# First batch of an attention-then-ReGLU kernel: first scores moved into the gate ring, z sums in banks of their own, two thirds of the gate-and-value table formed beside the first units

## Chip, cores, metric

One core of a Trainium2 chip. The time is the device time of a run in microseconds (us); the span in a profile is about 1.8 us shorter. Every run also has a mean granted TensorE clock.

## The reference, cut

```python
# x: 4 x 12416 x 128, inducing: 32 x 128 (m = 32)
def mab(q, kv):                       # softmax attention, scale = 1/sqrt(128)
    s = scale * (q @ kv.transpose(0, 2, 1))
    a = np.exp(s - s.max(-1, keepdims=True))
    a /= a.sum(-1, keepdims=True) + 1e-09
    return a @ kv
h = mab(I, x)                         # 32 summary rows of a batch
y = mab(x, h).reshape(49664, 128)
gate = np.maximum(y @ w_gate, 0.0)    # 128 x 1536
val = y @ w_val
out = (gate * val) @ w_out            # 1536 x 128
```

## The kernel before

The kernel never forms y. It forms h, folds h into the weights (hgv = h times w_gate and w_val, 1536 columns, made in three parts of 512), and multiplies hgv by the exps p of the second scores. The work after that goes in *slots*, one *unit* of 1024 gated columns a slot: two gate matmuls into two banks of the ring "g", two value matmuls into a two-bank tile of "v", two relus by ScalarE (ACT), one multiply gate times value by VectorE (DVE). Unit s of a pair needs columns 128 s to 128 s + 127 of hgv only. Batches 1 to 3 have their first phase hidden beside units of the batch before; batch 0 has nothing to hide behind, and its start is what the change is about. That first phase takes x in 14 parts as they land: cast to fp16, transpose by PE, first scores (inducing rows times x), their exp, and from the exps the z sums (the denominators of the softmax) and the h sums; hT is h over z, transposed. A "ring" is a set of PSUM banks taken in turn, "fillers" are matmuls whose result nobody reads. PE below is TensorE, POOL is GpSimd.

```python
def bank(tag, name, shape=None, dtype=FP32):          # eight PSUM banks in all
    return psum.tile(shape or [P, BLK], dtype, tag=tag, bufs={"g": 3, "v": 2, "o": 1}[tag], name=name)

z1_ps = bank("v", "z1_ps", [P, 2 * BLK])               # one two-bank tile for both z sums
z1a, z1 = z1_ps[:, 0 : 8 * M], z1_ps[:, BLK : BLK + M]
s1_ps = bank("v", "s1_ps", [P, 2, 2 * TPB, 2 * M])     # first scores: one two-bank tile, halves in turn
...
for j in range(n_parts + 3):                           # 14 parts of x as they land
    # cast of part j (POOL and ACT)
    if 1 < j < n_parts + 2:                            # scores and exp of part j - 2
        ps = s1_ps[:, j % 2, :, 0:M]
        for t in range(t0, t1):
            nc.tensor.matmul(ps[:, t - t0, :], xTs(xT, t, 1), indT, start=True, stop=True)
        nc.scalar.activation(out=p1[:, 0 : t1 - t0, :], in_=ps[:, 0 : t1 - t0, :], func=AF.Exp, scale=sm_scale)
    # z and h sums of part j - 3; turn(j): PE transpose into ring "g", DVE copy out of it
    ...
idle(idle_ps, 3, xT[0][:, 0:4, :].rearrange("p t c -> p (t c)"))   # filler matmuls
hT = finish_h(hT_ps, z1)                               # reciprocal of z, then h / z, on DVE
s2 = s2_pe(hT, xT, (0, 1, 0, 1)); p2 = s2_exp(s2)
ps = hgv_pe(hT, 0)                                     # four matmuls; then DVE copies two halves
for a in (0, BLK // 2):
    nc.vector.tensor_copy(out=hgv[:, a : a + BLK // 2], in_=ps[:, a : a + BLK // 2])
ps = bank("v", "hgv_ps", [P, 2 * BLK])
for k in (1, 2):
    hgv_pe(hT, k, ps[:, (k - 1) * BLK : k * BLK])
nc.vector.tensor_copy(out=hgv[:, BLK : 2 * BLK], in_=ps[:, 0:BLK])
nc.scalar.copy(out=hgv[:, 2 * BLK : DFF], in_=ps[:, BLK : 2 * BLK])
...
while True:                                            # the slots; "at" is the slot's number
    unit = next(todo_units, None); window.append(unit)
    ready = None if at == 10 else window.pop(0)        # values and multiply run a slot later, from 10 on two
    # gates of unit, values of ready, posted work, one filled-in event, output chain
    if 0 < at < 10:
        idle(idle_ps, 2, hgv[:, 0:BLK])                # two fillers a slot, meant to keep PE's clock up
    # relus of unit (ACT), multiply of ready (DVE)
    at += 1
```

The softmax here doesn't subtract the row's maximum and nothing guards it: scores larger than these inputs give would overflow.

## Time and profile before

Three runs gave 709.27 to 711.6 us, with a median of 710.46. The profile lines are in the prediction below; this table, from the busy time by stretches, gives what matters.

| stretch, us | PE | DVE | ACT | what goes on |
|---|---|---|---|---|
| 0 to 10 | 40% | 33% | 39% | x begins to land |
| 10 to 20 | 79% | 53% | 68% | casts, transposes, first scores, at the pace of x |
| 20 to 30 | 79% | 53% | 49% | h, hgv, first units |
| 30 to 40 | 99% | 87% | 90% | units, with 3.4 us at half clock |
| 60 to 700 | 91% | 99% | 98% | units at full pace |

To read it: from 40 us on DVE and ACT are full.

### The profile page before, as it was taken

The numbers are of one execution on the slowest core, as the hardware profiler recorded it, in microseconds if no ns is written. First come the engines' busy times: TensorE is split into PE (matmuls) and PEld (weight loads), VectorE is DVE, ScalarE is ACT, GpSimd is POOL, SyncE is SP. The second block draws the span as 40 slices with busy tenths as digits, with TensorE's granted clock in tenths as the row PEclk, the third lists the DMA queues.
The fourth block names the chain that finished last, engine by engine and source line by source line (L and its number), as shares of the span: only waits on it lengthen the run. The fifth ranks groups of instructions, "written<-read, shape, count | busy, mean of one in ns | idle before, by whom it ended". The sixth has DMA issues, their size and how long they took to land.

```text
span 709.0 us, 14077 instructions
## 1 busy us (share of the span) xinstructions
PE 637.9 (90%) x4626; PEld 186.0 (26%) x4626; DVE 678.9 (96%) x621; ACT 675.3 (95%) x1382; POOL 350.5 (49%) x646
## 2 busy tenths in 40 slices
PE   6899999999998999999998899999999898888997
PEld 5322222222222222222222222222222222222224
DVE  4599999999999999999999999999999999999997
ACT  5699999999999999999999999999999999999995
POOL 3661637535176546355256362852616443534543
PEclk9999999999999999999999999999999999999999
DMA  8657865431247867523139677653223132231222
GB/s 342 216 129 163 171 178 152 119 82 61 74 145 152 203 167 199 133 82 91 46 107 197 166 175 172 160 124 76 68 67 94 50 90 56 79 89 49 71 58 89
DMA packets 142346, 87.58 MB, mean 124 GB/s; under 512 B 117152, under 2 KB 125632, under 8 KB 139968
## 3 DMA queue, kind: packets, MB, share of 16 engines
q1 hardware_dynamic: 142272, 86.68, 47.2%
q8 instruction: 36, 0.59, 0.4%
q14 instruction: 38, 0.31, 0.1%
HBM read 27.80 MB, written 25.43 MB: 75 GB/s over the span
## 4 chain that ended last, share of the span: by engine, by line
ACT 32%; PE 29%; issue 17%; DVE 14%; DMA 6%; POOL 1%; SPq 1%; ACTq 0%; DVEq 0%
ACT g L961 23%; DVE gv L966 13%; PE o_ps L662 13%; PE v_ps L864 9%; ACT oT L668 5%; PE g_ps L864 4%; DMA gv<-in_x_dram 2%; ACT p2q L195 2%; DMA x<-in_moe_w_val_dram 1%; ACT p1T L527 1%; DMA out_dram<-osb 1%; DMA x<-in_x_dram 1%; PE h_ps L579 1%; POOL osb L679 0%; PE idle_ps L263 0%
## 5 line engine op out<-in xcount | busy, mean ns | idle before, releaser
L966 DVE TENSOR_TENSOR gv<-g,v_ps 128x1024 f16<-128x1024 f16 (+1 forms) x578 | 658.0, 1210 | 9.4 <-PE g_ps L864 5.9
L961 ACT ACTIVATE g<-g_ps 128x512 f16<-128x512 f32 x1164 | 604.0, 618 | 12.3 <-PE g_ps L864 8.5
L662 PE MATMUL o_ps<-gv,wo 128*128 128x512 f16 x1128 | 352.5, 384 | 43.9 <-ACT oT L668 43.9
L679 POOL TENSOR_SCALAR osb<-o,z2i 128x128 f32<-128x128 f16 x380 | 165.9, 453 | 276.0 <-DMA o<-oT 273.9
L864 PE MATMUL g_ps<-p,hgv 32*128 32x512 f16 x1152 | 284.4, 380 | 2.6 <-ACT g L961 1.9
L864 PE MATMUL v_ps<-p,hgv 32*128 32x512 f16 x1152 | 224.2, 384 | 9.5 <-DVE gv L966 7.9
L864 PEld LDWEIGHTS <-hgv 32*128 32x128 f16 x2400 | 69.5, 91 | 269.3 <-issue 264.7
L662 PEld LDWEIGHTS <-wo 128*128 128x128 f16 x1176 | 80.9, 97 | 211.8 <-issue 195.4
L435 POOL TENSOR_TENSOR z2i<-zt,minus 128x16 f32<-128x16 f32 (+3 forms) x31 | 73.2, 2366 | 0.3
L668 ACT CAST oT<-o_ps 128x512 f16<-128x512 f32 (+1 forms) x98 | 58.4, 596 | 0.0
L496 POOL CAST x<-x 128x2048 f16<-128x2048 f32 x18 | 34.0, 1890 | 18.3 <-DMA x<-in_x_dram 18.3
L428 POOL TENSOR_TENSOR zt<-zt 128x32 f32<-128x32 f32 (+5 forms) x124 | 35.1, 283 | 9.7
L428 POOL TENSOR_TENSOR zt<-p2T 128x256 f32<-128x256 f16 (+3 forms) x31 | 17.4, 563 | 25.9 <-DMA p2T<-p 15.2
L270 DVE COPY xT<-xT_ps 128x1024 f16<-128x1024 f16 (+1 forms) x13 | 8.4, 650 | 10.0 <-PE xT_ps L269 9.2
L269 PE MATMUL xT_ps<-eye,x 128*128 128x128 f16 x97 | 9.0, 242 | 5.5 <-POOL x L281 4.8
L282 ACT CAST x<-gv 128x512 f16<-128x512 f32 (+1 forms) x12 | 7.2, 597 | 6.9 <-DMA gv<-in_x_dram 6.9
L195 ACT ACTIVATE p2q<-s_ps 128x512 f16<-128x512 f32 x22 | 13.4, 610 | 0.0
L281 POOL CAST x<-gv 128x512 f16<-128x512 f32 (+1 forms) x12 | 7.2, 598 | 10.2 <-DMA gv<-in_x_dram 10.1
L527 ACT ACTIVATE p1T<-s1T_ps 128x512 f16<-128x512 f32 x18 | 11.1, 616 | 0.0
L179 PE MATMUL s_ps<-xT,hT 128*32 128x512 f16 x108 | 10.8, 392 | 0.2
L601 POOL TENSOR_TENSOR hp<-hp,hq 128x129 f32<-128x129 f32 (+1 forms) x18 | 8.3, 461 | 2.8 <-ACT hq L600 2.8
L966 DVE TENSOR_TENSOR gvr<-g,v_ps 128x512 f16<-128x512 f16 x12 | 8.0, 684 | 1.7 <-PE g_ps L864 1.7
(93 smaller groups left out, 159.1 us busy)
## 6 DMA issues: line engine op xcount, KB each, us to landing
out_dram<-osb SPq DMA_DIRECT2D x95, 256.0 KB, 2.2
x<-in_x_dram SPq DMA_DIRECT2D x18, 1024.0 KB, 6.0
gv<-in_x_dram SPq DMA_DIRECT2D x11, 512.0 KB, 7.5
p<-p2q SPq DMA_DIRECT2D x88, 64.0 KB, 2.0
o<-oT SPq DMA_TRANSPOSE x98, 2.3
x<-in_moe_w_out_dram SPq DMA_DIRECT2D x1, 768.0 KB, 9.2
gv<-in_x_dram SPq DMA_DIRECT2D x2, 256.0 KB, 10.5
x<-in_moe_w_gate_dram SPq DMA_DIRECT2D x1, 512.0 KB, 9.0
```

The source lines that it names most:

```text
L179: nc.tensor.matmul(ps[32 * r : 32 * r + 32, :], hT[:, 0:M], xTs(xT, blocks[r] * TPB, TPB), start=True, stop=True,)
L195: nc.scalar.activation(out=p2q, in_=ps, func=AF.Exp, scale=sm_scale)
L428: nc.gpsimd.tensor_tensor(out=dst, in0=v[:, :, :, 0:m], in1=v[:, :, :, m : 2 * m], op=ALU.add)
L435: nc.gpsimd.tensor_tensor(out=z2i, in0=v[:, :, :, 0], in1=minus1[:, 0 : n * g].rearrange("p (n g) -> p n g", n=n), op=ALU.pow,)
L496: nc.gpsimd.tensor_copy(out=s["x16"][:, t0:t1, :], in_=s["x32", q])
L527: nc.scalar.activation(out=p1T, in_=ps, func=AF.Exp, scale=sm_scale)
L662: nc.tensor.matmul(c["ps"][:, 0:w], wo[:, i, :], gv(i), start=(i == 0), stop=(i == NFF - 1))
L668: nc.scalar.copy(out=oT[:, 0:w], in_=c["ps"][:, 0:w])
L679: nc.gpsimd.tensor_scalar(out=osb[:, t, :], in0=o16[:, t, :], scalar1=zz, scalar2=zz, op0=ALU.mult, op1=ALU.mult,)
L864: nc.tensor.matmul(ps[:, cols], hgv[:, s * P : (s + 1) * P], p2, start=True, stop=True)
L961: nc.scalar.activation(out=g16[:, k * BLK : (k + 1) * BLK], in_=ps, func=AF.Relu)
L966: nc.vector.tensor_tensor(out=ready["dst"][:, a : a + w], in0=ready["g16"][:, a : a + w], in1=ready["v"][:, a : a + w], op=ALU.mult,)
```

## The change

Intent: take two waits out of the start. The scores no longer share one tile with their predecessors, nor the late z matmuls one with DVE's sum; and only the first third of hgv is made before the first unit, so that unit 0 doesn't wait for the last of w_val. Three fillers take the place of the hgv matmuls, to keep PE busy. The core of the diff (left out: the renaming in the z loop, the old `idle_ps` bank that goes, and the same `ev_hgv` put into the later batches):

```diff
-    z1_ps = bank("v", "z1_ps", [P, 2 * BLK])
-    z1a, z1 = z1_ps[:, 0 : 8 * M], z1_ps[:, BLK : BLK + M]
-    s1_ps = bank("v", "s1_ps", [P, 2, 2 * TPB, 2 * M])
+    z1a_ps = bank("v", "z1a_ps", [P, 2 * BLK])
+    z1a, idle_ps = z1a_ps[:, 0 : 8 * M], z1a_ps[:, BLK : 2 * BLK]
+    z1 = bank("v", "z1_ps", [P, M])
...
-            ps = s1_ps[:, j % 2, :, 0:M]
+            ps = bank("g", "s1_ps", [P, 8, M])
...
+            for t in range(n if j - 3 >= n_big else 0):          # all z matmuls, then all h matmuls
+                first, last = j - 3 == n_big and t == 0, end and t == n - 1
+                nc.tensor.matmul(z1, ones16, p1[:, t, :], start=first, stop=last)
...
-    ps = bank("v", "hgv_ps", [P, 2 * BLK])
-    for k in (1, 2):
-        hgv_pe(hT, k, ps[:, (k - 1) * BLK : k * BLK])
-    nc.vector.tensor_copy(out=hgv[:, BLK : 2 * BLK], in_=ps[:, 0:BLK])
-    nc.scalar.copy(out=hgv[:, 2 * BLK : DFF], in_=ps[:, BLK : 2 * BLK])
+    idle(idle_ps, 3, xT[0][:, 0:4, :].rearrange("p t c -> p (t c)"))
...
+    def ev_hgv(b, k, first, last):
+        def pe(at):
+            ps = hgv_pe(state[b]["hT"], k)                       # a bank of ring "g"
+            post[at + 1].append(lambda: hgv_evac(state[b]["hgv"], ps, k))   # by ACT
+        fill(first, last, pe)
+    ev_hgv(0, 1, 1, 1)
+    ev_hgv(0, 2, 4, 4)
...
-                    ev_s2_quad(b, qd, a + 4, a + 8)
+                    ev_s2_quad(b, qd, a + (4 if a else 12), a + (8 if a else 18))
...
-                ev_s2(b, (b, 1), (2, 3, 2, 3), 5, 8)
+                ev_s2(b, (b, 1), (2, 3, 2, 3), 7, 8)
```

More of the change, by code (lines that the diff above doesn't have):

```diff
@@ L307 @@
                 )
+            end = j == n_parts + 2
+            for t in range(n if j - 3 >= n_big else 0):
+                first, last = j - 3 == n_big and t == 0, end and t == n - 1
+                nc.tensor.matmul(z1, ones16, p1[:, t, :], start=first, stop=last)
             for t in range(n):
-                first, last = j == 3 and t == 0, j == n_parts + 2 and t == n - 1
-                if j - 3 >= n_big:
-                    nc.tensor.matmul(
-                        z1, ones16, p1[:, t, :], start=j - 3 == n_big and t == 0, stop=last
-                    )
+                first, last = j == 3 and t == 0, end and t == n - 1
                 nc.tensor.matmul(hT_ps, x16[:, t0 + t, :], p1[:, t, :], start=first, stop=last)
@@ L319 @@
         if j == n_parts:
-            idle_ps = bank("g", "idle_ps")
             z1s = st([P, M], FP32, "z1s", 1)
@@ L641, in act @@
                 for k in range(3):
-                    def mk(at, k=k):
-                        ps = hgv_pe(s["hT"], k)
-                        post[at + 1].append(lambda: hgv_evac(s["hgv"], ps, k))
-                    fill(at + 2, at + 9 + 3 * k, mk)
+                    ev_hgv(b, k, at + 2, at + 9 + 3 * k)
             post[at + 1].append(act)
```

## The prediction

> **What bounds the kernel now.** I read the page first, then the busy time by stretches, the chain of waits of the first 37 us, and each engine's own timeline from 20 to 37 us. The page's busy shares and the stretches say where time can be lost at all:
>
> ```profile
> PE 637.9 (90%) x4626; PEld 186.0 (26%) x4626; DVE 678.9 (96%) x621; ACT 675.3 (95%) x1382; POOL 350.5 (49%) x646
> ...
> L966 DVE TENSOR_TENSOR gv<-g,v_ps 128x1024 f16<-128x1024 f16 (+1 forms) x578 | 658.0, 1210 | 9.4 <-PE g_ps L864 5.9
> L961 ACT ACTIVATE g<-g_ps 128x512 f16<-128x512 f32 x1164 | 604.0, 618 | 12.3 <-PE g_ps L864 8.5
> ```
>
> ```profile
> 20.00:30.00 10.00, 7.92 (x117) 4.24 (x118) 5.26 (x11) 4.85 (x13) 6.99 (x12) 0.99 0.71 216
> 30.00:40.00 10.00, 9.90 (x58) 2.55 (x55) 8.65 (x8) 8.99 (x20) 4.09 (x5) 0.84 0.33 113
> 40.00:50.00 10.00, 9.32 (x55) 2.39 (x56) 9.89 (x9) 9.94 (x21) 8.38 (x15) 1.00 0.78 193
> ```
>
> Columns of the second: stretch, length, then busy us of PE, PE's weight loads, DVE, ACT and POOL, then the granted PE clock. From 36 us to the end DVE and ACT are both 98% busy (1.17 us a unit of 1024 gated columns): nothing in the diff touches that stretch, except that it may begin earlier. So the whole question is how much earlier the gating stream reaches its full pace. In before that is at 36.2 us: DVE starts units 0 to 5 at 28.65, 30.16, 31.74, 33.25, 34.76 and 36.23, then eight units in 9.40 us, 1.18 each. The chain of waits names what holds the first relu back to 27.95 (start, length, what):
>
> ```profile
> 15.52 9.44 DMA x<-in_moe_w_val_dram
> ...
> 25.01 1.05 POOL wv L326
> ...
> 26.10 0.62 PE hgv_ps L160 x6
> ...
> 26.75 0.70 DVE hgv L338
> ...
> 27.47 0.59 ACT hgv L339
> 28.06 0.51 ACT g L961
> ```
>
> The second and third parts of the gate-and-value table (hgv) wait for the last piece of w_val, then for its cast, four of their matmuls, a DVE copy, and an ACT copy that starts only when DVE's is done. ACT takes its work in order, so the relu of unit 0, which needs the first part of hgv only, stands behind all that. What follows is a second loss:
>
> ```profile
> 28.00:29.00 1.00, 0.39 (x2) 0.09 (x2) 0.35 (x1) 1.00 (x4) 1.00 (x2) 1.00 0.74 107
> 29.00:30.00 1.00, 1.00 (x7) 0.23 (x8) 0.93 (x2) 1.00 (x4) 0.77 (x4) 0.89 0.61 188
> 30.00:31.00 1.00, 1.00 (x9) 0.16 (x6) 0.84 (x1) 1.00 (x3) 0.84 (x3) 0.50 1.02 426
> 31.00:32.00 1.00, 1.00 (x7) 0.19 (x6) 0.65 (x2) 0.42 (x2) 1.00 (x1) 0.50 0.78 328
> 32.00:33.00 1.00, 1.00 (x6) 0.11 (x4) 0.96 (x1) 0.67 (x2) 0.22 (x2) 0.50 0.06 16
> 33.00:34.00 1.00, 1.00 (x11) 0.28 (x8) 0.75 (x1) 0.90 (x2) 1.00 (x1) 0.90 0.00 0
> ```
>
> PE idles from 27.24 to 28.61 (1.36 us, put down to ACT g), and from about 29.8 to 33.2 its granted clock is 0.50. In those 3.4 us the two filler matmuls of a slot take 0.96 us instead of 0.43, and the units come 1.5 us apart, set by PE.
>
> **What the Trainium skill says.** "TensorE: Matmul & The Clock Gate", section "Part 1: The HAM clock gate", says that the clock is halved after too idle a window of about 3.4 us, and that the windows run freely, not from the kernel's start. The trace agrees: one stretch of 3.4 us at 0.50, right after the least busy 3.4 us of PE. "PSUM — Partial Sum Buffer", section "PSUM bank collisions raise a hardware error", says that two engines may not be on one bank at once, even both reading, so software must order them. The trace shows an ordering coarser than that: the ACT copy of hgv waits for DVE's copy of another bank of the same two-bank tile. The first scores do so too, next.
>
> ```profile
> 22.40 0.25 PE L290 MATMUL s_ps<-indT,xT 128*128 128x32 f16 x4 [0.22 <-ACT p L292]
> ...
> 23.28 0.18 PE L311 MATMUL z_ps<-p,ones 128*128 128x32 f16 x1
> ...
> 24.28 0.36 DVE L146 RECIPROCAL rz<-z_ps 128x32 f32<-128x32 f32 x1 [1.05 <-PE hT_ps L314]
> 24.75 0.22 DVE L148 TENSOR_TENSOR hT<-hT_ps,rz 128x64 f16<-128x64 f32 x1
> ```
>
> Scores of a part wait for the exp of the part before (ACT, 21.96 to 22.34), though it reads the other half of the tile; the z matmuls at 23.28 wait for DVE's sum of the other bank (22.80 to 23.22).
>
> **The change, part by part.**
>
> (a) Scores in the gate ring, z in its own tile. Until about 21.5 us the phase is paced by x arriving: POOL waits 10.1 us and ACT 6.9 us for it, so nothing is gained there. The ring of three now has two takers a round; counting back three, the scores wait for the evacuation of the turned rows that they need anyway, and the turned rows wait for an exp that stands on ACT before the cast that they need anyway. No new wait. After 21.5 us I replay the tail: the scores of the last but one part start at 22.03 instead of 22.40; its exp follows the one before, 22.36 to 22.64; the last scores go at 22.75 instead of 23.07, their exp 23.00 to 23.28 (was 23.42 to 23.70); the fp32 z matmul after DVE's sum at 23.17, the last z matmuls about 23.5 to 23.6, finished at 23.76. With z ahead of the h matmuls, rz runs 23.80 to 24.16 and hT is done at 24.49, instead of 24.97: **0.5 us**.
>
> (b) Two thirds of hgv moved into slots 1 and 4. With hT at 24.49, s2 goes at 24.54 (was 25.02), its exp ends at 25.59, and the first half of the DVE copy of hgv ends about 25.6 (25.69 + 0.38 - 0.48). The three new filler matmuls (3 x 0.215 = 0.65 us) fit exactly from 24.97 to 25.62, so the gate matmuls of unit 0 go at 25.65, the relu at about 26.05, and DVE starts unit 0 about 26.7 instead of 28.65: **1.9 us, of which 1.45 are (b)**. The second part of hgv is now asked for only after the second relu, about 27.1, when wv (cast done at 26.05) is ready: the w_val transfer leaves the chain.
>
> (c) Start-up pace. ACT now has relus of 0.51 us each (six took 3.05 us), plus one evacuation of about 0.5 us in slots 2 and 5. PE is busy most of the time from 26 to 29 us, so I expect no stretch at half clock. Then, following ring and engines by hand: DVE units 0 to 5 start at 26.7, 28.65, 29.9, 31.1, 32.3 and 33.5: from unit 2 on DVE itself is the pace, at 1.22. Unit 5 is **2.7 us** earlier than its 36.23.
>
> (d) What is given back. DVE loses one copy of 0.69 us, and ACT gains it as one more evacuation (two instead of one, about 0.5 us of its pipe). The exp of s2 and of the quad (0.5 to 0.6 us each), done before unit 6 in the kernel before, now come in slots 8 and 13 to 19. So at unit 6 ACT has about 1.1 us more before it than at the same unit in before. If DVE alone bound from there, nothing of it would count; if ACT alone, all. From 36.02 us ACT gave 19 relus in 9.44 us, 0.50 each (one lasts 0.6, but the next starts inside it), so 1.0 us a unit against DVE's 1.18: over the ten units of slots 6 to 15, without an output chain to evacuate, that leaves ACT some 1.8 us in hand, enough for the 1.1; later the two engines are level. I charge **0.3 us**, for what ACT may not make up in time.
>
> Sum: 2.7 - 0.3 = 2.4 us. 710.46 - 2.4 = **708.1 us**, 0.34% less.
>
> **Rivals.**
>
> 1. ACT is the real bound after slot 6, so the postponed exps cost their full 1.1 us: gain 1.6, time 708.9. For it: ACT is 98% busy, level with DVE. Against: the 1.8 us in hand worked out above.
>
> 2. The clock falls anyway, because the windows run freely and the new order still makes PE wait for relus of 0.5 us. Then some three or four units come 1.5 us apart again: 3 to 4 x 0.3 = about 1 us back, time 709.1. Against it: seven banks of gates and hgv matmuls, three fillers and two more each slot keep PE streaming some 75% of 26 to 28 us by my replay, as against less than 60% of before's 26.4 to 29.8. The other way round, before may escape the low clock in some runs; its three times (709.27 to 711.6) spread by about that much.
>
> 3. The shared gate ring adds waits in the phase of loading, or the second part of hgv takes a bank that the relus need: 0.5 to 1 us lost, time about 709. The count above speaks against it.
>
> 4. Everything gained at the start is hidden by a later wait, on batch 1 say, and the time stays at 710.5. Against: from 36 us on no transfer holds DVE or ACT for long (DVE's gaps in all are 9.4 us, most of them at the start and the end), and the order of later work is the same.
>
> **Range and chances.** The replay gives 708.1; all the gain with no charge and a little more in the tail gives 707.0, and before's three runs lie 1.2 us either way of their middle. Two rivals together would make 709.8. Range 706.5 to 709.7. Two per cent is 14.2 us, nearly half of all that happens before the steady pace is reached, so neither faster nor slower by 2% is in sight: 0.98 for within, 0.01 each side.
>
> **What would show it.** Right: rz starting near 23.8, first relu near 26.05, first gv near 26.7, wv's cast no longer in the chain, granted clock 1.00 in each us of 26 to 36, DVE starting unit 5 near 33.5, and from there the same 1.17 us a unit. Wrong: hT not earlier (a); a relu still behind a hgv copy (b); a stretch at 0.50 after 26 us (c); DVE waiting for relus in slots 6 to 20, where before it ran at 1.18 (d). The sum is wrong if the lead at unit 5 is not still there at 100 us, or if a new wait appears in the load phase before 20 us.

## The result and the profile after

Four runs of the changed kernel: 708.74 to 709.77 us, median 709.05; four of the kernel before, beside them: median 710.53. Ratio 0.9981, 95% interval 0.9963 to 0.9999. (A ratio is the mean time of one kernel's fast runs over that of the other's of the same rounds, so not quite the ratio of the medians.) That is within the range and within 2%, but the gain is 1.5 us and not 2.4.

The start went much as forecast. The chain of waits of the changed kernel (start, length, what), from h on:

```profile
24.73 0.40 PE s_ps L179 x4
25.12 0.22 PE hgv_ps L160 x4
25.34 0.75 PE z1a_ps L263 x3
26.09 0.32 PE g_ps L864 x2
26.41 0.04 PE v_ps L864 x2
26.46 1.08 ACT g L961 x2
27.54 0.04 issue
27.59 0.40 PE hgv_ps L160 x4
```

The w_val transfer and its cast are gone from it. New in it are the three fillers (L263): they stand between the hgv matmuls and the first gate matmuls. DVE's timeline of the kernel before, then of the changed one (start, busy us, operation, count, idle time before):

```profile
28.65 1.29 DVE L966 TENSOR_TENSOR gv<-g,v_ps 128x512 f16<-128x512 f16 x2 [1.21 <-POOL wo L885]
...
36.23 6.94 DVE L966 TENSOR_TENSOR gv<-g,v_ps 128x1024 f16<-128x1024 f16 x6 [0.25 <-ACT p L190]
```

```profile
27.13 1.28 DVE L966 TENSOR_TENSOR gv<-g,v_ps 128x512 f16<-128x512 f16 x2 [0.98 <-ACT g L961]
29.09 9.21 DVE L966 TENSOR_TENSOR gv<-g,v_ps 128x1024 f16<-128x1024 f16 x8 [0.67 <-ACT hgv L170]
38.51 3.55 DVE L966 TENSOR_TENSOR gv<-g,v_ps 128x1024 f16<-128x1024 f16 x3 [0.21 <-PE g_ps L864]
```

The first multiply comes 1.52 us earlier, and from 29.09 on DVE goes at its own pace (eight in 9.21 us), where before it got there only at 36.23. The clock, by stretches of the changed kernel (columns as in the prediction), stays at 1.00 where before had 0.50:

```profile
29.00:30.00 1.00, 1.00 (x7) 0.30 (x6) 0.92 (x1) 1.00 (x3) 0.77 (x4) 1.00 0.74 279
30.00:31.00 1.00, 0.92 (x6) 0.28 (x5) 1.00 (x2) 1.00 (x3) 0.84 (x3) 1.00 1.02 434
31.00:32.00 1.00, 0.99 (x8) 0.31 (x9) 1.00 (x2) 1.00 (x3) 1.00 (x1) 1.00 0.51 205
```

Then I numbered DVE's gv and gvr multiplies in both traces (unit 0 counts twice, as it is done in two halves; 590 in all) and subtracted the start times. The lead is 1.52 us at number 0, 2.58 at number 6 (unit 5), 2.25 at number 10, and stays at 2.25 up to number 75, at 115 us. **Then it falls in sudden steps, right after numbers 75, 139, 203, 331, 395 and 523, to 1.68 us at the end.** The steps are 0.36, 0.35, 0.35, 0.06, 0.09 and 0.22 us; more than half of that is made up again within some 20 multiplies, so that 0.57 us is lost in all. All those numbers are 11 plus a multiple of 64 (at 267 and 459, the two left out of that series, there is no step). The prediction has nothing of the kind. One of these steps, in DVE's timeline of before and after:

```profile
184.46 5.79 DVE L966 TENSOR_TENSOR gv<-g,v_ps 128x1024 f16<-128x1024 f16 x5
190.67 3.78 DVE L966 TENSOR_TENSOR gv<-g,v_ps 128x1024 f16<-128x1024 f16 x3 [0.42 <-PE g_ps L864]
```

```profile
184.57 3.52 DVE L966 TENSOR_TENSOR gv<-g,v_ps 128x1024 f16<-128x1024 f16 x3
188.87 5.75 DVE L966 TENSOR_TENSOR gv<-g,v_ps 128x1024 f16<-128x1024 f16 x5 [0.77 <-PE g_ps L864]
```

The same multiply waits 0.77 us instead of 0.42, "for PE" in both. The name is only the last semaphore seen; why it takes 0.35 us more is the question.

### The profile page after: what moved, and what is told of

Read it like the earlier page. It is cut to its first block, busy times and chain, and to the rows that moved or that the text cites. A ratio compares the mean times of both kernels' runs of the same rounds, so it can differ in the third digit from the quotient of the medians.

```text
span 707.4 us, 14082 instructions
## 1 busy us (share of the span) xinstructions
PE 637.4 (90%) x4629; PEld 186.3 (26%) x4629; DVE 677.8 (96%) x620; ACT 675.7 (96%) x1383; POOL 348.7 (49%) x646
## 4 chain that ended last, share of the span: by engine, by line
ACT 32%; PE 29%; issue 18%; DVE 15%; DMA 4%; POOL 2%; SPq 0%; ACTq 0%; DVEq 0%; POOLq 0%
ACT g L961 23%; DVE gv L966 15%; PE o_ps L662 13%; PE v_ps L864 9%; ACT oT L668 5%; PE g_ps L864 4%; DMA gv<-in_x_dram 2%; ACT p2q L195 2%; ACT p1T L532 1%; DMA o<-oT 1%; PE h_ps L584 1%; POOL osb L679 1%; DMA out_dram<-osb 0%; PE hgv_ps L160 0%; PE o_ps L724 0%
```

## The experiments

Theories. **1**: the early start is most of the gain, and the later loss is chance. **2**: the later loss is lasting, at fixed places. **3**: the gain is mostly that before has a stretch at half clock. Twelve kernels ran; all were correct, all with five rounds. Two notes on the texts below: "unit 10" and the like in them are the numbers of DVE's multiplies; and "full clock" is a mean clock of 0.999 or 1.000 (the profiles at 0.999 have a low stretch only in the last microseconds), while 0.997 or 0.998 is one stretch of 3.4 us at half clock.

### The kernel before, unchanged, and the changed one again

Edit: none.

> The kernel before, unchanged, to see its own spread. Theory 1 (early start is most of the gain): its runs without a stretch at half clock (mean clock 1.000) still take about 710.0, its runs with one (0.998) about 711. Theory 3 (the gain is mostly before's stretch at half clock): runs at mean clock 1.000 take about 709.2, level with the changed kernel. Ratio to before within 0.1% of 1.

> The changed kernel again. Theory 1: about 709.0 (0.2% under before); the lead over before's profile is again 2.2 to 2.3 us from unit 10 to unit 75, and what is lost of it later (0.57 us in the first profile, at units 75, 139, 203, 523) falls at other sizes, as chance. Theory 2 (a lasting loss in fixed places): again 1.6 to 1.8 at the end, with the same steps at the same units.

Measured: before again 710.48 (ratio 0.9994, interval 0.9979 to 1.0009), changed again 709.49 (0.9982, 0.9968 to 0.9996). With all runs that have a clock:

| kernel | full clock | one low stretch (0.997, 0.998) | lower |
|---|---|---|---|
| before | 14 runs, mean 709.57 | 19 runs, 710.65 | 6 runs, 711.66 |
| changed | 6 runs, 708.96 | 4 runs, 709.90 | none |

(The first and the last call ran on chip 9, the second on chip 3; the full-clock runs of before were 709.46 to 709.92, 709.31 to 709.45 and 709.42 to 709.76 in them, so the chips differ by some 0.2 us.)

What follows: a low stretch costs the kernel before 1.1 us, and 25 of its 39 runs have one or more; the changed kernel has one in 4 of 10. At equal clock the change is worth only 0.6 to 0.75 us. So neither theory 1 nor theory 3 is right alone: of a difference of some 1.5 us in the medians, half is clock. And theory 1 is wrong on the later loss: the new trace has steps at the same numbers with the same sizes within 0.02 us. Theory 2 holds, without a cause yet.

### Scores alone, hgv alone

Edits: the changed kernel with hgv, and the slots of the second scores, as in before; and the kernel before with hgv and these slots as in the change.

```diff
# scores alone, against the changed kernel
-    idle(idle_ps, 3, xT[0][:, 0:4, :].rearrange("p t c -> p (t c)"))
+    ps = bank("v", "hgv_ps", [P, 2 * BLK])
+    for k in (1, 2):
+        hgv_pe(hT, k, ps[:, (k - 1) * BLK : k * BLK])
+    ...   # DVE copy, ACT copy
-    ev_hgv(0, 1, 1, 1)
-    ev_hgv(0, 2, 4, 4)
# hgv alone, against before: the same lines the other way round
```

> Part (a) alone: scores in the gate ring, z sums apart; hgv whole before the first unit as in before. Theory 1: hT about 0.45 us earlier against the last landing of x, but the w_val cast (about 25.0 to 26.05) still holds hgv's last two thirds, so the first relu stays at 27.9 to 28.0 and the time at 710.4, no gain. Rival: part (a) is worth its 0.5 us by itself, 710.0.

> Part (b) alone: two thirds of hgv in slots 1 and 4, phase 1 as in before. Theory 1: first relu about 26.8 (0.3 to 0.45 later than in the changed kernel), no stretch at half clock, 709.4. Rival: the first part of hgv too is held by something else once the scores wait for the exp, first relu over 27.3 and 710.

Measured: scores alone 710.73 (ratio 0.9998, interval 0.9985 to 1.0011): no gain, as theory 1 said. Its runs all have low stretches (four at 0.997 or 0.998, two at 0.995; whether the edit makes them likelier, six runs can't tell), so it compares only with before's low runs: 710.49 against 710.65. The expected time of the first relu could not be tested: its profile has a low stretch already at 20.2 us, in which hT comes 4.16 us after the last cast of x, and the first relu at 28.21. But that is 2.03 us after the end of the w_val cast, and in the four traces with before's hgv and phase 1 (before, before again, kept warm, one fewer) it is 1.90 or 1.91: the w_val cast holds it, as expected. hgv alone 709.55 (0.9985, 0.9972 to 0.9997): first relu at 26.77, as expected; at full clock 709.47, which is 0.1 under before and 0.5 over the whole change. So the scores' part needs the hgv part: without the late hgv the earlier hT waits for w_val. The reverse is not so: at DVE's multiply number 10 hgv alone is at 38.83, 0.69 us ahead of the kernel kept at full clock of the next section (39.52). It keeps only 0.1 of that because it has the later steps too, whose cause comes below. The profile of hgv alone has its one low stretch at 206.8 us, not at the start:

```profile
203.40:206.80 3.40, 2.52 (x28) 1.09 (x24) 3.40 (x4) 3.40 (x9) 2.45 (x3) 1.00 0.60 165
206.80:210.20 3.40, 3.40 (x14) 0.59 (x13) 3.01 (x4) 2.76 (x7) 1.73 (x4) 0.50 0.38 114
```

PE was busy for 2.52 of 3.4 us ahead of it. That is where the remainder of a batch (one tile of rows, in small units) is done, which none of the edits touches.

### Before, kept warm

```diff
+        if at == 0:
+            idle(idle_ps, 5, hgv[:, 0:BLK])
         if 0 < at < 10:
             idle(idle_ps, 2, hgv[:, 0:BLK])
```

> Before, with five filler matmuls (5 x 0.215 = 1.1 us) in slot 0, where PE idles from 27.2 to 28.6. Theory 1 and 3 both: no stretch at half clock, units 2 to 5 come 1.15 us apart instead of 1.5, so unit 5 about 1.2 us earlier at 35.0. Theory 1: time 1 us under before's throttled runs, about 709.7, still 0.6 over the changed kernel. Theory 3: level with the changed kernel, 709.0.

Measured: 709.58 (ratio 0.999, interval 0.9978 to 1.0002), four of five runs at full clock. Their mean, 709.55, is no better than before's own three runs at full clock in that call (709.31 to 709.45): the fillers gain the clock and nothing else. DVE's timeline:

```profile
28.71 6.03 DVE L968 TENSOR_TENSOR gv<-g,v_ps 128x512 f16<-128x512 f16 x6 [1.29 <-POOL wo L885]
34.99 8.07 DVE L968 TENSOR_TENSOR gv<-g,v_ps 128x1024 f16<-128x1024 f16 x7 [0.25 <-ACT p L190]
```

Unit 5 starts at 34.99 instead of 36.23: 1.24 us is what the low stretch costs the start. That is the size that was expected, and a clean base for the rest: at number 10 this kernel is at 39.52 and the changed one at 38.51, so at equal clock the change leads by 1.0 us there, of which 0.57 go later.

### The changed kernel without its three fillers

```diff
-    idle(idle_ps, 3, xT[0][:, 0:4, :].rearrange("p t c -> p (t c)"))
     state[0] = dict(x16=x16, xT=xT, hT=hT, hgv=hgv)
```

> The changed kernel without its three new fillers after the first hgv matmuls. Theory 1: gate matmuls of unit 0 0.2 us earlier (the fillers end at 26.03, the hgv half and the exp are done at 25.8), PE busy enough without them: no half clock in most runs, 708.9. Rival (clock): in some runs a stretch at half clock after 26 us, and about 1 us more in these.

Measured: 708.82 (ratio 0.9982, interval 0.9969 to 0.9996). Five runs at full clock have a mean of 708.79, and the first relu comes 1.62 us after hT instead of 1.78: the fillers cost 0.16. The sixth run has clock 0.994 and took 710.87, so something like the rival happens too; one run in six can't be called more or less than with fillers.

### Second third of hgv by DVE; second pair's scores later

```diff
# first: in ev_hgv
+            if (b, k) == (0, 1):
+                post[at + 1].append(
+                    lambda: nc.vector.tensor_copy(out=state[b]["hgv"][:, BLK : 2 * BLK], in_=ps)
+                )
+                return
# second
-                ev_s2(b, (b, 1), (2, 3, 2, 3), 7, 8)
+                ev_s2(b, (b, 1), (2, 3, 2, 3), 9, 9)
```

> The changed kernel with the second third of hgv evacuated by DVE (0.69 us) in DVE's gap of 0.67 us ahead of unit 1, not by ACT. If ACT is the bound in slots 0 to 9, as the changed kernel's back-to-back relus from 26.45 say: relus from unit 2 on 0.5 us earlier, the lead at unit 10 0.3 to 0.5 greater, about 708.6. If DVE binds there (rival): unit 1 later, nothing gained or 0.2 lost, 709.1.

> The changed kernel with the scores of the second pair asked for in slot 9, their exp in slot 10, in place of 7 and 8. If the fall of the lead from 2.6 to 2.25 at unit 9 is that exp's place in ACT's queue ahead of a DVE with nothing in hand: the fall comes later, and some of it is taken in by slots 10 to 15: lead at unit 20 2.3 to 2.5, time 0 to 0.3 lower. If ACT's work as such is the bound up to slot 16, the lead at unit 20 is 2.25 as before and the time the same.

Measured: by DVE 708.38 (ratio 0.9975, interval 0.9961 to 0.9988), and later scores 709.03 (0.9982, 0.997 to 0.9995). Of the first the time came out as expected and the reason did not: from number 0 to number 21 DVE needs 24.14 us in it, against 24.07 in the changed kernel's second trace, so taking a copy from ACT gains nothing at the start.

```profile
26.86 1.29 DVE L971 TENSOR_TENSOR gv<-g,v_ps 128x512 f16<-128x512 f16 x2 [0.98 <-ACT g L966]
28.07 0.68 DVE L458 CAST hgv<-hgv_ps 128x512 f16<-128x512 f32 x1
28.82 9.26 DVE L971 TENSOR_TENSOR gv<-g,v_ps 128x1024 f16<-128x1024 f16 x8
38.30 4.87 DVE L971 TENSOR_TENSOR gv<-g,v_ps 128x1024 f16<-128x1024 f16 x4 [0.22 <-PE g_ps L869]
```

With the exp in a later slot it is 24.06 us: nothing either. ACT is not the bound in slots 2 to 9; DVE is. **Where this version gained its 0.5 us (708.44 at full clock, against 708.90 for the later scores) was the later steps: it has none of them.** It has one DVE instruction more than the changed kernel, and so as many as before. That gave theory 2 a cause to test. In the traces, DVE's list of records (waits that stand as instructions of their own, and operations) has 1229 entries in before and 1228 in the change, and in steady work a unit is two entries, a wait and a multiply. The steps are 64 units apart: 128 entries. The trace also shows transfers of kind "instruction" in packets of 8192 bytes on queue 14, one of which starts near each of these places (629.2 us in the changed kernel's trace, where number 523 starts at 627.2 and the late one after it at 628.5). 8192 bytes over 128 is 64 bytes an entry. **Theory 2b**: DVE's instructions come in blocks of 128, and at the end of a block DVE can pause. Where the block ends after a multiply, the pause lies beneath the 1.2 us of that multiply; where it ends between a wait and its multiply, it is seen. One instruction fewer moves the end from one to the other.

### One DVE instruction more, two more; before with one fewer

```diff
# changed kernel, one more (two more: the memset twice, at columns 0 and 1)
     nc.vector.memset(ones16, 1.0)
+    pad = constp.tile([1, 4], FP32, name="pad")
+    nc.vector.memset(pad[:, 0:1], 0.0)
# before, one fewer
-    nc.vector.memset(ones32, 1.0)
+    nc.gpsimd.memset(ones32, 1.0)
```

> The changed kernel with one DVE instruction more: a memset of one element while DVE waits for x. Theory 2b (the later loss of 0.57 us is DVE's instruction stream: a block of 128 instruction records ends between a wait and its multiply in the changed kernel, whose DVE program is one shorter; in before it ends after the multiply): the steps at units 75, 139, 203, 331, 395 and 523 are those of before again, the lead of unit 10 lasts to the end, and runs at mean clock 0.999 or 1.000 take 708.4, 0.5 under the changed kernel's 708.95. Rival (the loss comes of the later placing of the second pair's scores, or of the lead itself shifting against other transfers): nothing changes, 708.95.

> The changed kernel with two DVE instructions more. Theory 2b: the blocks end between a wait and its multiply again, one unit earlier in the stream: the long steps come back, at units 74, 138, 202 or so, and runs at full clock take about 708.9. If only the count of instructions up to some size mattered, or nothing of the kind: as with one more.

> The kernel before with one DVE instruction fewer (the memset of ones32 given to GpSimd). Theory 2b: it takes on the changed kernel's long steps at units 75, 139, 203, 331, 395 and 523, and runs at full clock take 710.0 instead of 709.5. Rival: as before.

Measured: one more 708.44 (ratio 0.9977, interval 0.9965 to 0.9989), five runs of five at full clock with a mean of 708.49, 0.47 under the changed kernel's 708.96; two more 709.18 (0.9987, 0.9974 to 1.0), five of five too; before with one fewer 711.34 (1.0015, 1.0003 to 1.0027), whose runs with one low stretch take 711.29 against before's 710.65 (one run at full clock, 709.73, is too few to say; 710.0 was expected). DVE's timeline at the place shown above (number 140), for one more, for two more, and for before with one fewer:

```profile
188.12 6.06 DVE L968 TENSOR_TENSOR gv<-g,v_ps 128x1024 f16<-128x1024 f16 x5 [0.42 <-PE g_ps L866]
```

```profile
186.78 7.35 DVE L969 TENSOR_TENSOR gv<-g,v_ps 128x1024 f16<-128x1024 f16 x6 [0.31 <-ACT g L964]
```

```profile
191.05 3.48 DVE L966 TENSOR_TENSOR gv<-g,v_ps 128x1024 f16<-128x1024 f16 x3 [0.78 <-PE g_ps L864]
```

With one more, the idle time is back at 0.42 us. With two more there is a new gap one multiply earlier, 0.31 us, put down to an ACT relu. With one fewer, before has the 0.78 us of the change. All steps do the same: none with one more; after 74, 138, 202, 266, 394 and 522 with two more; after 75, 139, 203, 331, 395 and 523 for before with one fewer. Starts of DVE's multiplies by number, from the traces:

```
kernel                  DVE entries   no. 0   no. 6   no. 10   no. 21   last     21 to last
before                  1229          28.65   36.23   40.76    53.47    703.49   650.02
before, kept warm       1229          28.71   34.99   39.52    52.21    702.25   650.04
scores alone            1229          28.90   36.28   40.82    53.51    703.57   650.06
before, one fewer       1228          28.72   36.17   40.71    53.39    704.00   650.61
changed                 1228          27.13   33.65   38.51    51.22    701.81   650.59
changed, second trace   1228          26.83   33.35   38.21    50.90    701.51   650.61
later scores            1228          27.03   33.55   38.40    51.09    701.68   650.59
without fillers         1228          26.95   33.47   38.33    51.02    701.63   650.61
second third by DVE     1229          26.86   33.44   38.30    51.00    701.05   650.05
changed, one more       1229          26.84   33.36   38.22    50.91    700.99   650.08
changed, two more       1230          26.81   33.33   38.18    50.87    701.58   650.71
```

The last column is the work from 50 us on. In these traces it goes with the count of DVE's entries and with nothing else that was varied: 650.02 to 650.08 us for 1229, 650.59 to 650.71 for 1228 and 1230. (hgv alone, 1228 entries, is left out because of its low stretch at 206.8 us, though it has the same steps. Before again and the last kernel below have 1229 entries, 650.07 and 650.05.) So the later loss is shown to come from where DVE's instruction stream stands, and some 0.57 us is its price.

The traces also show the pause itself. Count DVE's entries from 0: the six late multiplies of the changed kernel are entries 191, 319, 447, 703, 831 and 1087, those of two more 191, 319, 447, 575, 831 and 1087, all of them 63 plus a multiple of 128. In before and in one more the first six of these places hold a wait. From the end of a wait's entry to the start of its multiply, where DVE is free, it is 0.04 to 0.05 us; at the six places of the changed kernel it is 0.40. (At entry 63, at 42.16 us, it is 0.46, but there DVE is idle no longer than in before, 0.10 us.) So the pause is 0.35 us each time, and it comes after the wait. What is seen of it depends on when the wait ended: at number 331 it ended 0.42 us before the multiply then running did, and 0.06 us is left; at 75, 139 and 203 it ended after that multiply or 0.13 us before it, and all is seen. What DVE does in the pause stays open. It is no wait for the packet named above: in the changed kernel a packet of 8192 bytes starts 0.67 to 0.90 us after each of the six late multiplies has begun.

### Both, as a better version

Edit: the last two edits to the changed kernel, the DVE copy and the later scores, together.

> The best version so far (second third of hgv by DVE, 708.38) with the second pair's scores in slots 9 and 10 as well. Its DVE program is as long as before's, so no long steps. Lead at unit 20 over e7 0.1 or none: 708.2 to 708.4. Rival: the later exp costs, 708.6.

Measured: 708.56 (ratio 0.9981, interval 0.9969 to 0.9993); three runs at full clock 708.29 to 708.56, two with a low stretch 709.31 and 709.41. No better than the DVE copy alone, as the DVE timelines had it. The best versions beside both kernels are the change with one DVE instruction more and the one with DVE's copy, at 708.4.

## Why the prediction was right or wrong

**Within the range, but 0.95 us above its point: the sum lacked a term, and one of its terms is not always there.** The range says little for the mechanism, as rivals 1 to 3 (708.9, 709.1, about 709) lie in it too, and nearer to the result than the sum. By its own steps:

- (a) 0.5 us: right. From the end of the last cast of x to hT it is 3.75 us in before and 3.29 in the change, 0.46 less, the same within 0.01 in all seven traces that have the edit and no low stretch ahead of it. That it is worth nothing alone is shown by the scores alone. In the first profile hT was only 0.30 earlier, because x landed 0.16 later.
- (b) 1.9 us at the first multiply: measured 1.52. Of the difference, 0.16 is x landing later and 0.16 the three fillers, which I had said fit exactly in 0.65 us; they take 0.75 on the chain and did hold the gate matmuls. The w_val transfer left the chain as said.
- (c) Unit 5 2.7 us earlier, at 33.5: measured 2.58, at 33.65. That it came so near is in part luck: unit 1 was 0.44 us late (29.09 for 28.65), and DVE's pace from there was 1.14 us a unit where I had 1.22. No low stretch from 26 to 36 us: right in the profile. But the kept-warm kernel shows that 1.24 us of this lead is the low clock of before, and 25 of its 39 runs have a low stretch, 14 none (where in the run, only the traces tell); and rival 2 was right too in part, as 4 of 10 runs of the change have a low stretch somewhere (where, no trace of these runs shows).
- (d) 0.3 us given back: the size was right (2.58 to 2.25) and the cause wrong. I put it down to postponed work on ACT. The copy given to DVE and the later scores both left it as it was. It is one step, 1.43 us instead of 1.13, between numbers 9 and 10, in all versions with hgv in the slots. That is where the order of the slots changes (no values in slot 10), and I take it that a DVE which keeps up feels it, while in before the loss is already taken earlier (in the kept-warm kernel number 5 to 6 takes 1.47 us, in the change 1.13); this is argued and not shown.
- **The step that failed is the sentence "nothing in the diff touches that stretch, except that it may begin earlier".** The diff took one DVE copy away, and with it moved all later instructions of DVE by one place, so that pauses of 0.35 us after some waits show: 0.57 us lost from 115 us on, a quarter of the lead. With one idle memset at the start to restore the count, the median is 708.44, within 0.35 of the 708.1 predicted; some of that nearness is luck, as the median of before in that call stood at 709.72 and not at 710.46. Rival 4, a later loss of the gain, had the right stretch, but took all of the gain and named a wait for batch 1, which did not occur.
- Rival 1 (ACT the bound, 708.9) came near in time with a cause that the runs refute. Rival 3 (about 709) did not occur in the phase of loading: hT follows the last cast as replayed. Its other half is real: with hgv's second part in the gate ring, DVE needs 1.96 us from number 0 to number 2, and 1.38 in the kept-warm kernel; but the replay had that (26.7 to 28.65).
- Four readings in the prediction do not hold. At full clock a pair of fillers takes 0.54 us in the view that gives 0.96 at half clock (28.98 in the chain of before), not 0.43. "Eight units in 9.40 us, 1.18 each" counts the last multiply to its end: from start to start it is mostly 1.13 or 1.14, so ACT had less in hand than 1.8 us. 14.2 us is 39% and not nearly half of the first 36.2. And the stretch at half clock does not follow "the least busy 3.4 us of PE": another one of the same trace was no busier, and the clock stayed at 1.00 after it (columns as before):

```profile
16.10:19.50 3.40, 1.99 (x46) 1.87 (x47) 1.06 (x3) 1.52 (x5) 0.95 (x3) 1.00 1.03 390
26.40:29.80 3.40, 2.04 (x18) 0.41 (x12) 1.89 (x4) 2.33 (x5) 2.44 (x4) 1.00 0.43 88
```

So the 1.7 us between the two profiled spans are 1.0 us of earlier start at equal clock, 1.24 us of low clock avoided, less 0.57 us: 1.7.

## What to carry to other kernels

Before explaining a difference of a few tenths of a per cent, sort the runs by their granted clock: half of this gain was how often PE fell to half clock, and one median can't tell. Subtract the start times of the same instruction in two traces, all along the run: a lead that falls in steps at equal distances need not be a wait in the program, whatever releaser the profile names. And where an engine is the bound, adding or removing a single instruction ahead of a long unrolled stretch can change its pace; try one more harmless instruction before giving up a change as worthless.

## What the Trainium skill lacked or had wrong

- "Runtime: NRT & Kernel Launch", section "Instruction fetch mechanics", has instructions refilled in 16 KiB blocks of 256, with the cost of a block's end mostly hidden. The places found here are 128 entries apart on DVE, with 8192-byte instruction packets near them (packets of 16384 bytes are there too, on another queue; whether the block size is a setting, no run tests), and when such a place lies between a wait and its operation the cost shows: up to 0.36 us each, 0.57 us in all, in the traces with 1228 or 1230 DVE entries.
- "TensorE: Matmul & The Clock Gate", section "Part 1: The HAM clock gate": the low stretches of 3.41 us at 0.50 agree. That section ties them to idle windows; here they followed 3.4 us in which the profile has PE busy for 2.04 us (kernel before) and 2.52 us (hgv alone, amid full-pace work). It has no figure for how busy is busy enough, and PE's busy time alone does not give one: after 1.99 us (kernel before, 16.1 to 19.5) and 2.52 us (the changed kernel's second trace, 202.6 to 206.0) the clock stayed at 1.00. In one kernel 25 of 39 runs had a stretch and 14 none, at a cost of 1.1 us.
- "PSUM — Partial Sum Buffer", section "PSUM bank collisions raise a hardware error", speaks of banks and quadrants. In this kernel the waits came by whole tiles, two banks together; the edit that split the tiles, and put the z matmuls ahead of the h matmuls, took 0.46 us out of the chain. No page has such waits.
